# Delta rule and feed-forward on one core: chunk 0's substitution of four units in one ring instead of two pairs

## The chip, the cores and the metric

The kernel runs on one core of one Trainium2 chip. The metric is the time of one execution on the device, in microseconds (us). A core has a matrix engine (TensorE, PE in the profile; PEld is its loading of weights), VectorE (DVE), ScalarE (ACT), GpSimd (POOL) and SyncE (SP), which in this kernel only issues copies. GpSimd and ScalarE issue copies too. [...]

## What is computed

The inputs are q, k, v of 4 batches, 8 heads, 768 steps and 48 features, a step size beta for each step, and two weight matrices in 64-bit floats, w_in (384 x 2048) and w_out (2048 x 384). The reference, cut to what matters:

```python
k_n = k / (norm(k, axis=-1) + 1e-06)
state = zeros(B, H, D, D)
for t in range(S):
    y[:, :, t] = q[:, :, t] @ state                      # before the update
    v_old = k_n[:, :, t] @ state
    state += beta[:, :, t] * outer(k_n[:, :, t], v[:, :, t] - v_old)
x = y, with the heads side by side                       # (B*S, 384)
h = x @ w_in
out = (h * sigmoid(1.702 * h)) @ w_out                   # (3072, 384), f32
```

The recurrence is along the 768 steps; heads and batches are independent.

## The kernel before

The steps are cut into 6 chunks of 128. A chunk of one batch, with its 8 heads, is a unit; there are 24, numbered so that units 0 to 3 are the four batches of chunk 0, 4 to 7 those of chunk 1, and so on. Two units of neighbouring batches form a pair, whose 256 rows go through the feed-forward together.

Inside a chunk the recurrence becomes a triangular system. For each unit the kernel needs these things:

- Keys: `load` (line 84) fetches them, `normalize_first` or `normalize_mixed` (line 317) divides them by their norms: a square on ScalarE, a sum on VectorE, a power on GpSimd, then a product on VectorE. `turn` (line 385) transposes them on TensorE (psT, copied to kT), and `gram` (line 362) multiplies them with themselves (psG, copied to G).
- The inverse of the four 32 x 32 diagonal blocks of each head. `prepare` (line 389) writes the blocks of G to device memory (Nd) and gathers them again, so that each of the 128 partitions of NT holds one block of one unit. `invert` (line 444) then inverts all of them at once by a long row of products and sums on VectorE, scales them by beta (YS), and sends them through device memory (Yd) to tiles XB, in which TensorE can use them. Chunk 0 has its own way to NT: `diagonal` (line 428) computes only the diagonal blocks, and the code at lines 906 to 921 writes and gathers them.
- Scores: `scores` (line 558) transposes the queries and multiplies them with the keys (psT, psQ, copied to QS and M); `select` zeroes the upper triangle of M on GpSimd.

The substitution of a unit has four blocks (`blk`, 32 rows each). `solve` multiplies the values V of a block with the inverse (psU), `solved` copies the result to U on ScalarE, `below` multiplies U with the blocks of G below (psR), and `rest` subtracts that from V on VectorE. `together` (line 786) issues one set: the solves and the belows that it is given, head by head in turns on TensorE, then the copies, then the subtractions. Behind it, `queries` and `outputs` make the unit's rows of x (psY) and the state for the next chunk, and copy both out; the features that lie in other partitions are moved by six small copies on SP (xT<-last) once a pair is complete.

The feed-forward has two stages: `hidden` (line 693) computes x @ w_in (ph) and its gelu (gT), two features blocks of 128 at a time, and yields twice in each; `written` and `both_written` multiply with w_out (po). The weights come as 64-bit floats. `fetch_in` and `fetch_out` load them in pieces, w_in in four quarters of the features, and `conversions` (line 255) turns them into 32-bit floats with five instructions on VectorE and one on ScalarE for each piece; `fill(n)` issues n steps of it. `warm(n)` (line 132) issues n matmuls whose result is not used.

The order of the instructions is written out by hand: `pinned` (line 100) keeps nearly all in the order of the code. In the stage around the change (lines 933 to 1045) it is this:

1. Chunk 0 is inverted (line 945) while the scores of its four units are made. Sixty unused matmuls are tied to the end of the inversion by a memset (line 510).
2. Units 0 and 1 are substituted by `hops`: eight sets in which the two units take turns. Behind each set come one step of conversion, one step of the generator `keys` and eleven or three unused matmuls (lines 988 to 992). Their outputs follow, then the loads of the keys of units 7 and 8.
3. Units 2 and 3 are substituted in the same way, and `hidden` of the first pair runs between their sets. `keys` (line 964) prepares the keys of units 4 to 8 in steps during both.
4. `hidden` of the second pair is put behind that of the first; chunk 1 is inverted (lines 1033 to 1042) while `feed` issues the rest of x @ w_in.
5. From line 1047 on, `woven` takes the units of the later chunks one by one and weaves feed-forward work between them.

Of the kernel before, what the change touches and what calls it, by code (L numbers as in the profile page):

```python
# [18 lines left out]
def kernel(  # L19
# [21 lines left out]
    B, H, S, D = q.shape  # L41
# [15 lines left out]
    XR = DP - D  # L57
    NW, NA, NY, NU = 80, 3, 60, 11
    NQ = DFF // 4
# [71 lines left out]

    def warm(n, after=None):
        ps = ps_moe.tile([128, 256], F32, tag="moe", name="ps_warm")
        if after is not None:
            after(ps[:, 0:1], 0.0)
        for _ in range(n):
            pe.matmul(ps, lhsT=ones[:, 0:128], rhs=ones, start=True, stop=True)
# [35 lines left out]

    def fetch_in(i, other=None):

        f = slice(i * NQ, (i + 1) * NQ)
        raw = quarter(i if i < 3 else 4)
        for j in range(KC):
            for p, r, m, step in x_rows:
                (other if other and p >= DP else sync)(  # L180
                    out=as_rows(raw[j])[p : p + m, 0],
                    in_=moe_w_in[r + j * step : r + j * step + m, f],
                )
# [71 lines left out]
    def conversions():  # L255
# [27 lines left out]
    fetches = {  # L283
        ("in", 0, 1): lambda: fetch_in(3),
        ("in", 1, 1): lambda: (fetch_out(4), fetch_out(5), fetch_out(6), fetch_out(7)),
# [158 lines left out]
    def invert(c, b0=0, nb=B):  # L444
# [55 lines left out]
        for i in range(0, HS, Q):  # L500
# [7 lines left out]
            yield 0.0  # L508
        if c == 0:
            warm(NY, vec.memset)  # L510
        YS = wk.tile([128, BS, BS], F32, tag="P", name="YS")[part]
# [26 lines left out]
    class Step:  # L538
# [6 lines left out]
        def __init__(self, n, xT):  # L545
            self.c, self.b = units[n]
            self.xT = xT
            self.kn, self.kT, self.G = ready.pop(n)
            self.qp = QP[n % len(QP)]
            self.n, self.V = n, loaded.pop(n)  # L550
            self.US = late_U if n == B - 1 else US[n % len(US)]
            self.U = self.US[:, 0 : H * D].rearrange("p (h d) -> p h d", h=H)
            self.scored = self.scores()
# [4 lines left out]
        def scores(self):  # L558

            c, S = self.c, slice(128, 128 + D)  # L560
            self.QS = (
                spare("QS")[:, 0 : NP * (128 + D)].rearrange("p (j t) -> p j t", j=NP) if self.n == B - 1
                else wk.tile([128, NP, 128 + D], F32, tag="QS", name="QS", bufs=3)
            )
            transposed(self.qp, self.QS[:, :, 0:128])
            if c > 0:
# [3 lines left out]
            self.M = (  # L570
                spare("M").rearrange("p (h t) -> p h t", h=H) if self.n in (B - 1, B + 1)
                else wk.tile([128, H, 128], F32, tag="M", name="M", bufs=3)
# [119 lines left out]

    def hidden(xT, gT, t, cost):

        n = t.stop - t.start
        for f0 in range(0, FC, 2):
            if f0 // FQ == len(gT):
# [87 lines left out]

    def together(solves, belows):

        solves = [(X, blk) for X, blk in solves if X]
        belows = [(X, blk) for X, blk in belows if X]
        psU = bank("psU") if solves else None  # L790
        psR = bank("psR") if belows else None
        for h in range(H):
            for X, blk in solves:
                X.solve(blk, h, psU)
            for X, blk in belows:
                X.below(blk, h, psR)
        for X, blk in solves:
            X.solved(blk, psU)
        for X, blk in belows:
            X.rest(blk, psR)  # L800
# [89 lines left out]
    for i in range(B, len(KN)):  # L890
# [8 lines left out]
        for name in ("blocks", "others")  # L899
    ]  # L900
    quarter(2)
    late_U = spare("U")[:, 0 : H * D + XR]
    pool.memset(late_U[:, H * D :], 0.0)
    Nd = dram.tile([B * H * C * BS], F32, tag="Nds", name="Nd", bufs=1)
    turn(0)
    for b in range(B):
# [4 lines left out]
        if b % 2 == 1:  # L911
            for e in range(2):
# [3 lines left out]
                )  # L916
            d = slice((b - 1) * NB * H, (b + 1) * NB * H)
            sync(
                out=NT[d].rearrange("d i k -> d (i k)"),
                in_=Nd.rearrange("(d r) -> d r", r=BS * BS)[d],  # L920
            )
    pool.tensor_copy(landed[64:], NT[64:, 0, 0:1])
    for b in range(B):
# [12 lines left out]
    pair = [new_step(n) for n in range(B)]  # L936
    inverting = invert(0)
    for n in range(B):
        next(pair[n].scored)
        warm(NA)  # L940
        run(pair[n].scored)
# [21 lines left out]

    def keys():

        def unit(n):
            yield from normalize_mixed(n)
            yield from prepare(n)

        begun[2 * B] = prepare(2 * B)  # L970

        def first(n):
            yield from normalize_mixed(n)
            next(begun[n])

        work = [unit(n) for n in range(B, 2 * B)] + [first(2 * B)]
        for t in range(26):
            for u, begin in enumerate((0, 3, 6, 14, 17)):
                s = t - begin
                if s >= 0 and s % 2 == 0:  # L980
                    next(work[u], None)
            yield
        for w in work:
            run(w)
# [12 lines left out]
    load(8, ((KN, k),), sync)  # L997
    for n in range(B, B + 2):
# [82 lines left out]
```

## Time and profile before

| what | us |
|---|---|
| median of three runs | 794.65 (794.42 to 795.07) |
| the profiled execution | 796.73 |
| its span on the core | 795.0 |
| TensorE busy | 759.3 |
| VectorE busy | 459.0 |
| ScalarE busy | 239.8 |
| GpSimd busy | 123.3 |

The span is the time from the first to the last instruction of the core. Busy time says how long an engine had something in hand, not that it was needed then. In a row of the timeline, the bracket at the end gives the time for which the engine had stood idle before and the instruction that ended the wait. A copy is shown on the queue that issued it; it lands later.

### The profile page before, as it was taken

How to read it: one execution, taken by the hardware profiler on the slowest of the kernel's cores; microseconds unless marked ns; L12 is line 12 of the kernel's file. 1: busy time of each engine (PE TensorE's matmuls, PEld its weight loads, DVE VectorE, ACT ScalarE, POOL GpSimd, SP SyncE). 2: the span in 40 equal slices, each digit the busy share in tenths (PEclk: the TensorE clock that was granted, in tenths of full speed). 3: DMA queues.
4: the chain of work that ended last, by engine and by line, in shares of the span. 5: the costliest groups of instructions: out<-in, count | busy, mean ns of one | idle time of the engine just before them, and what ended most of it. 6: DMA issues, size and time to landing. Idle time of an engine off the chain costs nothing.

```text
span 795.0 us, 18695 instructions
## 1 busy us (share of the span) xinstructions
PE 759.3 (96%) x8083; PEld 567.4 (71%) x8083; DVE 459.0 (58%) x945; ACT 239.8 (30%) x521; POOL 123.3 (16%) x128
## 2 busy tenths in 40 slices
PE   9679999878899999999999999999999999999998
PEld 7457778645668768768768768668678678677684
DVE  5796667998797656656666666666756530100000
ACT  4432563234333323223223323223223223121120
POOL 4112320001222211211212212212210000000000
PEclk9678899999999999999999999999999999999999
DMA  6968462064334223222222231231230020000000
GB/s 124 147 122 187 120 132 65 13 173 103 89 79 94 54 62 65 55 68 59 54 69 58 55 86 41 64 89 29 64 86 12 21 43 1 12 16 1 26 0 20
DMA packets 139329, 52.81 MB, mean 66 GB/s; under 512 B 113824, under 2 KB 134432, under 8 KB 139248
## 3 DMA queue, kind: packets, MB, share of 16 engines
q1 hardware_dynamic: 136976, 43.70, 25.1%
q0 software_dynamic: 2176, 7.67, 3.8%
q8 instruction: 63, 1.03, 0.6%
q10 hardware_dynamic: 96, 0.26, 0.1%
q14 instruction: 18, 0.15, 0.1%
HBM read 33.13 MB, written 17.30 MB: 63 GB/s over the span
## 4 chain that ended last, share of the span: by engine, by line
PE 78%; DVE 14%; DMA 4%; issue 1%; ACT 1%; SPq 1%; DVEq 0%; POOL 0%; ACTq 0%; POOLq 0%
PE po L102 28%; PE ph L102 25%; PE psY L102 6%; PE psU L102 5%; DVE P L102 4%; PE ps_warm L102 3%; PE psQ L102 3%; DVE YB L102 3%; PE psG L102 3%; PE psT L102 2%; PE psR L102 2%; DVE w_out L102 2%; DVE NT L102 2%; DVE tmp L102 1%; SPq L102 1%
## 5 line engine op out<-in xcount | busy, mean ns | idle before, releaser
L102 PE MATMUL po<-w_out,gT 128*128 128x384 f32 x768 | 264.7, 492 | 5.9 <-DVE w_out L102 5.2
L102 PE MATMUL ph<-xT,w_in 128*128 128x256 f32 x1152 | 261.8, 383 | 3.2 <-ACT gT L102 2.8
L102 PEld LDWEIGHTS ph<-xT,w_in 128*128 128x128 f32 x1152 | 214.7, 190 | 36.0 <-ACT gT L102 4.7
L102 PEld LDWEIGHTS po<-w_out,gT 128*128 128x128 f32 x768 | 140.7, 190 | 96.5 <-DVE w_out L102 8.0
L102 DVE TENSOR_TENSOR V<-V,psR 64x384 f32<-64x384 f32 (+1 forms) x96 | 53.3, 556 | 197.2 <-PE psR L102 195.9
L102 ACT ACTIVATE gT<-ph 128x512 f32<-128x512 f32 x96 | 56.3, 596 | 136.6 <-PE ph L102 136.5
L102 DVE TENSOR_TENSOR P<-NT,YB 64x8 f32<-64x8 f32 (+31 forms) x190 | 88.8, 467 | 5.3
L102 ACT COPY US<-psU 32x384 f32<-32x384 f32 x92 | 43.2, 469 | 146.7 <-PE psR L102 130.0
L102 DVE TENSOR_REDUCE YB<-P 64x4 f32<-64x8 f32 (+31 forms) x190 | 80.9, 426 | 6.5
L102 PEld LDWEIGHTS psU<-V,XB 32*32 32x32 f32 x1536 | 58.7, 107 | 34.6 <-issue 26.7
L102 PE MATMUL psU<-V,XB 32*32 32x48 f32 x1536 | 69.8, 205 | 0.7 <-issue 0.3
L598 POOL TENSOR_SCALAR_AFFINE_SELECT M<-M 128x1024 f32<-128x1024 f32 x20 | 26.1, 1305 | 262.3 <-DVE M L102 168.8
L102 PE MATMUL psR<-US,G 32*32 32x48 f32 x2208 | 62.0, 205 | 1.6 <-issue 1.6
L102 PE MATMUL ps_warm<-ident 128*128 128x256 bf16 x275 | 44.4, 320 | 13.2 <-ACT G L102 7.2
L102 PEld LDWEIGHTS psR<-US,G 32*32 32x32 f32 x2208 | 52.3, 106 | 2.8 <-issue 2.3
L102 PEld LDWEIGHTS <-ident 128*128 128x128 bf16 x275 | 29.6, 113 | 22.0 <-issue 12.7
L102 PE MATMUL psQ<-QS,kT 48*128 48x176 f32 (+1 forms) x384 | 34.9, 322 | 1.1 <-ACT QS L102 1.1
L102 DVE TENSOR_TENSOR P<-NT 64x256 f32<-64x256 f32 (+7 forms) x40 | 33.7, 842 | 0.3
L102 DVE TENSOR_REDUCE NT<-P 64x64 f32<-64x1024 f32 (+7 forms) x40 | 32.6, 815 | 1.4
L87 POOL DMA_DIRECT2D KN<-in_k_dram x15 | 14.2, 947 | 112.2 <-PE psY L102 103.3
L102 PEld LDWEIGHTS psQ<-QS,kT 48*128 48x128 f32 x384 | 28.6, 192 | 4.0 <-ACT QS L102 2.4
L102 PE MATMUL psG<-kT 48*128 48x128 f32 x384 | 30.5, 303 | 0.2
(96 smaller groups left out, 602.0 us busy)
## 6 DMA issues: line engine op xcount, KB each, us to landing
Nd<-G SPq DMA_DIRECT2D x16, 512.0 KB, 3.5
QP<-in_q_dram SPq DMA_DIRECT2D x24, 192.0 KB, 3.7
V<-in_v_dram SPq DMA_DIRECT2D x24, 192.0 KB, 3.2
out_dram<-o SPq DMA_DIRECT2D x24, 192.0 KB, 2.1
XB<-Yd SPq DMA_DIRECT2D x24, 128.0 KB, 3.1
KN<-in_k_dram POOLq DMA_DIRECT2D x15, 192.0 KB, 3.8
Yd<-YS SPq DMA_DIRECT2D x22, 128.0 KB, 2.4
NT<-Nd SPq DMA_DIRECT2D x20, 128.0 KB, 2.6
```

The costliest lines, as they stand in the source:

```text
L87: dma(out=dst[n % len(dst)][:, :, 0:D], in_=src[b, :, c * C : (c + 1) * C, :].rearrange("h p d -> p h d"),)
L102: return lambda *a, **kw: tc.keep_in_program_order(op(*a, **kw))
L598: (pool if self.n < B else nc.gpsimd).affine_select(out=self.M, in_=self.M, compare_op=ALU.is_gt, fill=0.0, base=0, pattern=[[0, H], [1, 1 ...
```

## The change

- Chunk 0's four units are substituted in one ring of 16 sets: set i solves block i // 4 of unit i % 4, and multiplies and subtracts what set i - 2 solved. `together` takes something to issue between the copies and the subtractions (`beside`): one step of conversion in every fourth set, and in others a step of the preparation of the keys of units 4, 5 and 6, by the table `aside`.
- The outputs of units 0 to 3 follow sets 13, 14 and 15 and the ring. No unused matmuls stand between the sets; 90 stand before the last part of chunk 0's inversion, without the memset.
- The turns and products of the keys of units 4, 5 and 6 follow the ring, and only then come the loads of the keys of units 7 and 8. Units 7 and 8 are prepared between the steps of x @ w_in.
- `hidden` takes a range of features. Both pairs run behind the ring, first features 0 to 7 of each, then 8 to 15. The number of steps that `feed` issues during the inversion of chunk 1 is changed accordingly.
- Chunk 0's blocks are gathered into NT by one copy for all four units instead of two for two each.
- Quarters 2 and 3 of w_in are fetched through GpSimd's queue, quarter 2 directly behind quarter 1 and quarter 3 at set 12, instead of through SP behind the inversion and behind the conversion of quarter 0.
- The buffers of unit 3 (U, QS, M) are taken from the spare buffers at once, ahead of those for quarter 2.

The diff, without its changed constants (NW, NA, NY = 80, 3, 90; NU is gone):

```diff
-    def warm(n, after=None):
+    def warm(n):
         ps = ps_moe.tile([128, 256], F32, tag="moe", name="ps_warm")
-        if after is not None:
-            after(ps[:, 0:1], 0.0)
...
-    def fetch_in(i, other=None):
+    def fetch_in(i, other=None, only=False):
...
-                (other if other and p >= DP else sync)(
+                (other if other and (only or p >= DP) else sync)(
...
     fetches = {
-        ("in", 0, 1): lambda: fetch_in(3),
...
-        if c == 0:
-            warm(NY, vec.memset)
...
-            self.US = late_U if n == B - 1 else US[n % len(US)]
+            self.US = late["U"][:, 0 : H * D + XR] if n == B - 1 else US[n % len(US)]
...
-    def hidden(xT, gT, t, cost):
+    def hidden(xT, gT, t, cost, part=range(0, FC, 2)):
 
         n = t.stop - t.start
-        for f0 in range(0, FC, 2):
+        for f0 in part:
...
-    def together(solves, belows):
+    def together(solves, belows, beside=iter(())):
...
         for X, blk in solves:
             X.solved(blk, psU)
+        for _ in beside:
+            pass
         for X, blk in belows:
             X.rest(blk, psR)
...
+    late = {name: spare(name) for name in ("U", "QS", "M")}
     quarter(2)
-    late_U = spare("U")[:, 0 : H * D + XR]
...
-            d = slice((b - 1) * NB * H, (b + 1) * NB * H)
-            sync(
-                out=NT[d].rearrange("d i k -> d (i k)"),
-                in_=Nd.rearrange("(d r) -> d r", r=BS * BS)[d],
-            )
-    pool.tensor_copy(landed[64:], NT[64:, 0, 0:1])
+    sync(out=NT.rearrange("d i k -> d (i k)"), in_=Nd.rearrange("(d r) -> d r", r=BS * BS))
+    pool.tensor_copy(landed, NT[:, 0, 0:1])
...
     fetch_in(1, other_queue)
+    fetch_in(2, other_queue, True)
     fill(6)
...
+    warm(NY)
     run(inverting)
-    for s in pair:
+    for s in four:
         s.select()
-    fetch_in(2)
     fill(5)
-
-    def hops(a, b):
-
-        yield [(a, 0)], []
-        for blk in range(NB - 1):
-            yield [(b, blk)], [(a, blk)]
-            yield [(a, blk + 1)], [(b, blk)]
-        yield [(b, NB - 1)], []
...
-    preparing = keys()
-    path = hops(*pair[:2])
-    for i in range(2 * NB):
-        together(*next(path))
+    norms = {n: normalize_mixed(n) for n in range(B, 2 * B + 1)}
+    begun.update((n, prepare(n)) for n in range(B, 2 * B + 1))
+
+    def tick(*ns):
+        for n in ns:
+            if next(norms[n], True):
+                next(begun[n], None)
+
+    aside = [(), (4,), (), (4,), (), (4, 5), (), (5,), (), (5, 6), (), (6,), (), (6,), (), ()]
+    for i in range(B * NB):
+        j = i - 2
+        together(
+            [(four[i % B], i // B)],
+            [(four[j % B], j // B)] if j >= 0 and j // B < NB - 1 else [],
+            iter([fill(1) if i % 4 == 2 else tick(*aside[i])]),
+        )
+        if i >= B * NB - 3:
+            put_out(four[i - (B * NB - 3)])
+        if i == 12:
+            fetch_in(3, other_queue, True)
+    put_out(four[3])
+    for n in (4, 5, 4, 6, 5, 6):
+        tick(n)
         fill(1)
-        ahead_of(preparing, 1)
-        warm(NU if i < 6 else NA)
-    for s in pair[:2]:
-        put_out(s)
-        fill(1)
-    load(7, ((KN, k),), sync)
-    load(8, ((KN, k),), sync)
+    for n in (7, 8):
+        load(n, ((KN, k),), sync)
...
-    ffn.append(hidden(xTs[0], gTs[0], slice(0, NTH), 1.3))
-    path = hops(*pair[2:])
-    for i in range(2 * NB):
-        together(*next(path))
-        if i > 2:
-            feed()
-        else:
-            warm(NU // 2)
-        fill(2)
-        ahead_of(preparing, 2)
+    for part in (range(0, FC // 2, 2), range(FC // 2, FC, 2)):
+        for i in range(2):
+            ffn.append(hidden(xTs[i], gTs[i], slice(0, NTH), 1.3, part))
+    xTs.pop(0), xTs.pop(1)
+    aside = [(7, 4), (5,), (7, 6), (8,), (7,), (8,), (7,), (8,), (7,), (8,), (7,)]
+    for i in range(16):
+        feed()
+        fill(2 if ("in", 3, 1) not in done else 0)
+        if i < len(aside):
+            tick(*aside[i])
         if 3 <= i < 6:
             fetch_out(i - 3)
-    for s in pair[2:]:
-        put_out(s)
-        feed()
-        fill(2)
-    ffn.append(hidden(xTs[1], gTs[1], slice(0, NTH), 1.3))
-    xTs.pop(0), xTs.pop(1)
-    run(preparing)
...
-        feed(2 if i >= 16 else 1 - i % 2)
+        feed(1 if i >= 16 or i % 3 == 2 else 0)
```

More of the change, by code (lines that the diff above doesn't have):

```diff
@@ L57 @@
     XR = DP - D
-    NW, NA, NY, NU = 80, 3, 60, 11
+    NW, NA, NY = 80, 3, 90
     NQ = DFF // 4
@@ L561, in scores @@
             self.QS = (
-                spare("QS")[:, 0 : NP * (128 + D)].rearrange("p (j t) -> p j t", j=NP) if self.n == B - 1
+                late["QS"][:, 0 : NP * (128 + D)].rearrange("p (j t) -> p j t", j=NP) if self.n == B - 1
                 else wk.tile([128, NP, 128 + D], F32, tag="QS", name="QS", bufs=3)
@@ L570, in scores @@
             self.M = (
-                spare("M").rearrange("p (h t) -> p h t", h=H) if self.n in (B - 1, B + 1)
+                (late["M"] if self.n == B - 1 else spare("M")).rearrange("p (h t) -> p h t", h=H)
+                if self.n in (B - 1, B + 1)
                 else wk.tile([128, H, 128], F32, tag="M", name="M", bufs=3)
@@ L900 @@
     ]
+    late = {name: spare(name) for name in ("U", "QS", "M")}
     quarter(2)
-    late_U = spare("U")[:, 0 : H * D + XR]
-    pool.memset(late_U[:, H * D :], 0.0)
+    pool.memset(late["U"][:, H * D : H * D + XR], 0.0)
     Nd = dram.tile([B * H * C * BS], F32, tag="Nds", name="Nd", bufs=1)
@@ L935 @@
         warm(NA)
-    pair = [new_step(n) for n in range(B)]
+    four = [new_step(n) for n in range(B)]
     inverting = invert(0)
     for n in range(B):
-        next(pair[n].scored)
+        next(four[n].scored)
         warm(NA)
-        run(pair[n].scored)
+        run(four[n].scored)
         warm(NA)
@@ L962, in put_out @@
         steps.pop(s.n)
[L964 to L984, printed above, removed]
-    preparing = keys()
-    path = hops(*pair[:2])
-    for i in range(2 * NB):
-        together(*next(path))
-        fill(1)
-        ahead_of(preparing, 1)
-        warm(NU if i < 6 else NA)
-    for s in pair[:2]:
-        put_out(s)
-        fill(1)
-    load(7, ((KN, k),), sync)
-    load(8, ((KN, k),), sync)
+    norms = {n: normalize_mixed(n) for n in range(B, 2 * B + 1)}
[19 more added lines that the diff above has]
+        tick(n)
+        fill(1)
+    for n in (7, 8):
+        load(n, ((KN, k),), sync)
     for n in range(B, B + 2):
```

## The prediction

> **What bounds the kernel now.** I read the busy slices first, then the stretches by stage, then the chain of waits around the place that the change touches, then the timeline of VectorE and of the two queues there. In the page:
>
> ```profile
> span 795.0 us, 18695 instructions
> PE   9679999878899999999999999999999999999998
> DVE  5796667998797656656666666666756530100000
> ```
>
> TensorE is full from about slice 10 (200 us) to the end, so the kernel ends when TensorE got its long tail started. What decides when the tail starts lies before 200 us. Here are the stretches (columns: stretch; length; busy time and instructions of TensorE, its weight loads, VectorE, ScalarE, GpSimd; granted clock; DMA share; GB/s):
>
> ```profile
> 64.80:90.60 25.80, 24.23 (x478) 19.20 (x478) 14.96 (x28) 8.77 (x20) 3.90 (x3) 0.80 0.48 114
> 90.60:119.30 28.70, 26.76 (x500) 21.48 (x500) 20.15 (x40) 18.27 (x36) 9.28 (x11) 1.00 0.72 173
> 129.60:157.00 27.40, 24.78 (x126) 21.23 (x125) 26.02 (x54) 7.22 (x15) 1.41 (x1) 1.00 0.00 1
> 165.30:205.00 39.70, 33.68 (x364) 21.18 (x364) 33.92 (x72) 17.23 (x36) 4.16 (x3) 1.00 0.51 138
> 300.00:700.00 400.00, 399.77 (x4442) 299.67 (x4438) 228.68 (x480) 112.36 (x247) 64.73 (x52) 1.00 0.22 51
> ```
>
> From 129.6 to 157 VectorE works 26.0 of 27.4 us: that is the inversion of chunk 1. Behind it VectorE converts w_out and TensorE waits for it (33.7 of 39.7 us). So from 129.6 to about 205 VectorE sets the pace, and then TensorE has no slack (399.8 of 400). A later start of the inversion is therefore a later end, nearly one for one. Why it starts at 129.6 is in VectorE's and SP's timelines (start, us, what, idle before and who ended it):
>
> ```profile
> 124.56 0.96 DVE L102 SCALAR_TENSOR_TENSOR w_in<-tmp,w_in 128x768 f32<-128x768 f32 x1
> 129.59 1.23 DVE L102 TENSOR_TENSOR NT<-NT,bI 128x1024 f32<-128x1024 f32 x1 [4.07 <-DMA NT<-Nd]
> ```
> ```profile
> 94.48 1.17 SPq L102 DMA_DIRECT2D KN<-in_k_dram  x2
> 114.85 1.90 SPq L102 DMA_DIRECT2D Nd<-G  x4
> 119.86 0.31 SPq L102 DMA_DIRECT2D NT<-Nd  x1
> 120.22 1.96 SPq L102 DMA_DIRECT2D Nd<-G  x4
> 126.02 0.52 SPq L102 DMA_DIRECT2D NT<-Nd  x1
> ```
>
> VectorE has nothing left and waits 4.07 us for the last blocks (NT) of unit 7, the last of chunk 1. They took the whole way: keys loaded at 94.5, normalized, turned, multiplied, written (Nd), gathered (NT). **The question is when that way ends in the changed kernel.** The chain of waits shows what the old substitution cost:
>
> ```profile
> 64.84 0.79 PE psU L102 x16
> 67.75 1.31 PE ps_warm L102 x11
> 71.55 1.57 issue
> 77.34 2.46 PE ps_warm L102 x11
> ```
>
> Its sets of pair 0 run at a pace set by eleven dummy matmuls each: 1.31 us at full clock (119 ns each), 2.46 us at half (224 ns).
>
> [...] in pair 0 the clock stayed halved for about 10 us (73.8 to 84.4) although TensorE was hardly idle[...]
>
> **The change part by part**, in time of the profiled execution: 796.73 us, of which the span is 795.0. The runs' median is 794.65, 2.1 under it.
>
> *Gather of chunk 0 in one copy.* NT was fetched in two copies of 256 KB (median 3.7 us); four of 128 KB took 2.9. So 0.8 us per 128 KB gives 5.3 us for 512 KB, an estimate. SP issues the last Nd write some 0.5 us sooner, as the early gather at 21.6 is gone: landing at about 25.9 + 5.3 = 31.2 instead of 30.3. Inversion 0 and all behind it, up to XB at 64.8, come 1.0 us later: 65.8 (bounds 64.8 if size costs nothing, 67.3).
>
> *Fetches moved from SP to GpSimd.* Quarter 2: 12 issues of some 0.5 us (6 took 2.99) on GpSimd, behind quarter 1, in its 23.3 us of idling before the gate; the 1.5 MB fill DMA time idle from 52 to 58.5. Nothing; without that cover up to 2 us on XB. Quarter 3: 12 issues at set 12, behind the last pow of the ring; needed at E+24 below, so nothing; GpSimd's next work behind it, four fetches of w_out and the pow of unit 7 at E+19, comes later than it lands.
>
> *ph in halves.* Both pairs' features 0 to 7 come first, 48 matmuls that need only quarters 0 and 1 of w_in; quarters 2 and 3 are converted meanwhile. As many matmuls as before, so nothing, as long as VectorE's conversions (E+36 below) end ahead of their use at about E+38. The spare buffers named earlier, and the memset of 0.06 us that leaves VectorE: nothing, no step waits for them.
>
> *Dummy matmuls.* 87 leave the substitution (14.5 us busy from 64.8 to 119.3). The 90 that replace the pinned 60 no longer wait for VectorE: they start at 51.3 and last 90 x 0.119 = 10.7 us, to 62. TensorE then stands 3.8 us, so the ring starts at half clock.
>
> *The ring.* A set takes TensorE 0.8 us at full and 1.43 at half clock (75.84 to 77.27). Sets 0 and 1: 2 x 1.43 = 2.9. Each set with block 0 has two updates on VectorE (1.14) and a fill or part of a normalization ahead of it (mean of 0.96, 0.54, 0, 0.93 is 0.61): 4 x 1.75 = 7.0. Blocks 1 and 2: VectorE 0.56 + 0.61 is under 1.43, so 8 x 1.43 = 11.4. Sum 21.3, at 87.1 (full clock: VectorE's 1.2 rules, 17.5). Four outputs with sets 14 and 15: 1.4 us each (64 rows, 2.81 for two), and the third and fourth bank must be emptied by ScalarE (1.4 us): 8.6 at full, 12.6 at half clock; I take 10.4. The ring ends at E = 97.5 (bounds 91 and 101). Before, pair 1's last output ended at 119.3, so substitution is 22 us shorter; but 82 of 192 matmul records of ph (0.22 us each) were done by 129.6, and the keys of chunk 1 were prepared in its gaps.
>
> *From E to the inversion of chunk 1.* In the new order the last three units' psT and psG stand behind the ring, and keys of unit 7 are loaded behind all 12 Nd writes on SP, where before they were loaded at 94.5, ahead of them. The queries and values of units 4 and 5 stand behind these keys; they are first used in the inversion, and have 20 us.
> 1. Turn and multiply units 4, 5, 6 through two ps_big buffers, TensorE and ScalarE by turns (psT 0.6, kT 0.6, psG 1.1, G 1.08, three times, first after 1.4 of xT copies): 10.3 at full, 13.5 at half clock; 11.5.
> 2. Nd of unit 6 on SP 2.1, keys land 4.6 (median; 3.5 to 6.8): E+18.2.
> 3. ScalarE has the square of unit 7 ahead of the first gelu: 0.52, table load 1.28, gelu 0.60: E+20.6. TensorE filled both ps_moe buffers (12 matmuls) by E+17 and stands. The 9 ph matmuls ahead of psT of unit 7: 4.0 at full, 8.0 at half; 5.0: E+25.6. The normalization (0.54 + 1.66 pow + 0.93) hides under them, at E+23.
> 4. psT 0.6, six ph 2.65, psG 1.1: E+30.0. ScalarE's gelu, one conversion and G: 1.3: E+31.3.
> 5. Four Nd writes to landing 5.1 (114.85 to 119.9), NT 3.5: E+39.9.
> VectorE's 25 fills and the keys of 7 and 8 end at about E+36, so they hide; 4 us is their margin.
>
> The inversion starts at 97.5 + 39.9 = 137.4 instead of 129.6: **+7.8 us**. Behind it nothing new: ph still to do is some 21 us (24.4 before), over by E+63, before the first po at 29.5 us behind the inversion's start (159.2 before); the 3 us saved go into idling. The profiled execution would take 804.5 (span 802.8), and the median, 2.1 under it, **802.5 us**.
>
> **Rivals.**
> *Small loss.* The clock holds through the ring (E about 92 to 94), then +2 to +5: 797 to 800. For it: the outputs of pair 0 ran at full clock (2.81 for two). Against: the dummies are gone.
> *Large loss.* Half clock to the first ph, keys at 6.8 us, a late psG: terms 1 to 3 at their upper ends add 2 + 2.2 + 3 and the ring 3 to the 7.8, 18 in all: 813.
> *Faster.* The new order does what it removes: with E = 92 and lower ends (10.3 + 1.9 + 3.5 + 2.4 + 4.0 + 4.2 + 1.2 + 5.0 + 2.9 = 35.4) the inversion starts at 127.4: 792.5. It decides once E plus the way is under 128. For it: SP no longer waits for each unit's Nd before the next (5.4 us per unit from 103.5 on). Against: it needs all lower ends at once.
> *No change.* Inversion at 128 to 131.2, midway: 794.5.
>
> **How the numbers follow.** Forecast (+5 to +12) 0.45, small loss 0.22, large loss 0.18, no change 0.06, faster 0.09. Within 0.2% (1.6 us) is about what a measurement of this kernel can't tell from no change. Slower by more: 0.85; within 0.06; faster 0.09. The range leaves 0.1 at each end: 795.5 to 811. The forecast's own range is 799.5 to 806.5.
>
> **What would show it.** NT<-NT,bI of chunk 1 at about 137, released by the copy of NT; VectorE idle 3 to 5 us ahead of it. Keys of unit 7 issued on SP near 111, behind 12 Nd writes. Ring sets 1.4 us apart with a clock near half; last output near 97. A gap on TensorE after 12 ph matmuls, ended by gelu. Wrong if the way of unit 7 is under 33 us, or if po takes over the start of the tail because ph is done earlier than VectorE's conversions allow.

## The result: slower, and the profile after

The changed kernel takes 808.28 us (median; runs from 806.47 to 809.76), beside 794.86 us for the kernel before on the same chip: a ratio of 1.0164, with a 95% interval of 1.0135 to 1.0194. It is slower by 13.4 us. The forecast was 802.5 us, within 795.5 to 811. The measured time lies inside that range, but outside the forecast's own part of it (799.5 to 806.5), between it and the large loss.

The profiled execution took 806.47 us, 1.8 under its kernel's median; the one of before lay 2.1 over its own. So the two traces differ by less than the medians do: the spans by 9.6 us. The two traces can explain only that; the rest is taken up below.

The page of the changed kernel, the span and the busy slices of TensorE and VectorE with the granted clock:

```profile
span 804.6 us, 18577 instructions
...
PE   9697959878899999999999999999999999999998
...
DVE  5886447999797667567666666656656630100000
...
PEclk9676588999999999999999999999999999999999
```

What is new lies in slices 4 to 6: the clock (PEclk, in tenths) reads 6, 5 and 8 there, where it was 8, 8 and 9 before, and TensorE has a dip in the sixth slice (101 to 121 us). The stretches show both (columns as before: stretch; length; busy time of TensorE, weight loads, VectorE, ScalarE, GpSimd; clock; DMA share; GB/s):

```profile
66.00:90.00 24.00, 20.32 (x623) 18.85 (x624) 16.03 (x32) 8.81 (x19) 10.17 (x14) 0.52 0.17 43
90.00:100.00 10.00, 9.90 (x125) 9.29 (x122) 1.97 (x5) 3.50 (x12) 0.78 (x2) 0.61 0.35 75
...
110.00:120.00 10.00, 3.03 (x13) 2.39 (x12) 1.49 (x3) 2.94 (x5) 1.77 (x1) 0.74 1.09 162
120.00:139.10 19.10, 19.10 (x92) 16.12 (x92) 14.79 (x25) 9.01 (x16) 4.27 (x6) 0.87 0.62 142
139.10:167.00 27.90, 24.14 (x122) 20.30 (x120) 26.25 (x53) 6.62 (x14) 1.59 (x1) 1.00 0.00 1
...
300.00:700.00 400.00, 399.78 (x4410) 300.19 (x4407) 234.73 (x483) 114.46 (x250) 68.19 (x54) 1.00 0.23 53
```

The ring (66 to 90) and its outputs (90 to 100) run at about half clock. From 110 to 120 all three compute engines stand: TensorE works 3.0 of 10 us, VectorE 1.5, ScalarE 2.9. From 139 on the picture is that of before again: the inversion of chunk 1 on VectorE, 26 of 28 us. VectorE's timeline gives its start:

```profile
134.00 0.96 DVE L102 SCALAR_TENSOR_TENSOR w_in<-tmp,w_in 128x768 f32<-128x768 f32 x1
134.88 0.35 DVE L102 TENSOR_SCALAR tmp<-raw 128x384 int32<-128x384 int32 x1
139.16 1.23 DVE L102 TENSOR_TENSOR NT<-NT,bI 128x1024 f32<-128x1024 f32 x1 [3.93 <-issue]
```

The inversion starts at 139.16 instead of 129.59, 9.57 us later, and the span is 9.6 us longer. From its start to the end of the span it is 665.4 us in both traces. So behind the start of the inversion this execution took as long as that of before, and all that was lost was lost ahead of it. The bracket names no releaser here (`issue`); the next lines show that the blocks of unit 7 came last. SP's timeline shows their way:

```profile
93.90 10.49 SPq L102 DMA_DIRECT2D xT<-last  x12
104.48 9.11 SPq L102 DMA_DIRECT2D Nd<-G  x12
113.69 1.02 SPq L102 DMA_DIRECT2D KN<-in_k_dram  x2
...
131.67 2.81 SPq L102 DMA_DIRECT2D Nd<-G  x4
135.82 0.31 SPq L102 DMA_DIRECT2D NT<-Nd  x1
```

The gather of its blocks is issued at 135.82, and the fastest of the four gathers of chunk 1 takes 3.3 us to land, which gives 139.1, when the inversion starts. Its keys are issued at 113.69 (94.48 before), behind twelve copies of x and twelve block writes. ScalarE's timeline shows what waits for them:

```profile
117.03 0.52 ACT L102 ACTIVATE ksq<-KN 128x384 f32<-128x384 f32 x1 [8.95 <-DMA KN<-in_k_dram]
117.57 1.28 ACT L102 ACT_TABLE_LOAD   x1
118.86 0.60 ACT L102 ACTIVATE gT<-ph 128x512 f32<-128x512 f32 x1
```

ScalarE waits 8.95 us for these keys. The first gelu of x @ w_in is queued behind the square of unit 7 and runs at 118.86, though all matmuls of ph issued so far had ended at 112.55, and TensorE, whose two ph buffers are full, stands for 6.97 us until that gelu has emptied one. In TensorE's timeline each matmul of ph is two records (1152 in the whole trace for the kernel's 576), so the 24 records are the 12 matmuls that fill both buffers:

```profile
107.10 5.45 PE L102 MATMUL ph<-xT,w_in 128*128 128x256 f32 x24
119.52 6.88 PE L102 MATMUL ph<-xT,w_in 128*128 128x256 f32 x18 [6.97 <-ACT gT L102]
```

### The profile page after: what moved, and what is told of

Same layout as the page of the kernel before. It is cut to its first block, busy times and chain, and to the rows that moved or that the text cites. A ratio compares the mean times of both kernels' runs of the same rounds, so it can differ in the third digit from the quotient of the medians.

```text
span 804.6 us, 18577 instructions
## 1 busy us (share of the span) xinstructions
PE 763.6 (95%) x8026; PEld 575.6 (72%) x8026; DVE 458.5 (57%) x944; ACT 240.1 (30%) x521; POOL 137.0 (17%) x152
## 4 chain that ended last, share of the span: by engine, by line
PE 76%; DVE 14%; DMA 5%; issue 2%; ACT 2%; SPq 1%; DVEq 0%; POOL 0%; ACTq 0%; POOLq 0%
PE po L102 28%; PE ph L102 25%; PE psY L102 6%; PE psU L102 5%; DVE P L102 4%; PE psQ L102 3%; PE psR L102 3%; DVE YB L102 3%; PE psG L102 2%; PE psT L102 2%; DVE w_out L102 2%; DVE NT L102 2%; DMA Nd<-G 1%; DVE tmp L102 1%; DMA KN<-in_k_dram 1%
## 5 line engine op out<-in xcount | busy, mean ns | idle before, releaser
L102 PEld LDWEIGHTS psU<-V,XB 32*32 32x32 f32 x1536 | 63.8, 112 | 34.0 <-issue 27.6
L102 PE MATMUL psU<-V,XB 32*32 32x48 f32 x1536 | 74.4, 212 | 3.0 <-issue 1.7
L102 PE MATMUL psR<-US,G 32*32 32x48 f32 x2208 | 64.5, 210 | 1.4 <-ACT US L102 0.9
L102 PEld LDWEIGHTS psR<-US,G 32*32 32x32 f32 x2208 | 54.9, 110 | 3.0 <-ACT US L102 1.3
L102 PE MATMUL ps_warm<-ident 128*128 128x256 bf16 x218 | 31.6, 303 | 8.6 <-ACT G L102 7.2
L102 PEld LDWEIGHTS <-ident 128*128 128x128 bf16 x218 | 22.7, 107 | 13.9 <-issue 8.2
```

The lines of the kernel that those rows point to most:

```text
L102: return lambda *a, **kw: tc.keep_in_program_order(op(*a, **kw))
```

## The experiments

Each was run beside the kernel before on the same chip; the groups used four chips. The median of before lay between 793.3 and 795.9 us, so ratios are compared, not times across groups of runs. "Start" is the start of the inversion of chunk 1 in the profiled execution: 129.59 before, 139.16 after.

### Unit 7's keys earlier

```diff
         if i >= B * NB - 3:
             put_out(four[i - (B * NB - 3)])
+        if i in (13, 14):
+            load(i - 6, ((KN, k),), sync)
...
-    for n in (7, 8):
-        load(n, ((KN, k),), sync)
```

> The changed kernel, with one edit: the loads of the keys of units 7 and 8 are issued by SP right behind the outputs of units 0 and 1 (about 89 and 93 us), ahead of the copies of x and of the twelve Nd writes, instead of at 113.7. Theory A (the way of unit 7's keys starts the inversion of chunk 1 late): the square of unit 7 no longer waits at 117 but runs at 108, the stand of TensorE behind 12 ph matmuls (7.0 us) is gone, the inversion starts at about 130 instead of 139.2, and the time falls by 8 to 10 us to 798.5 to 800. Theory B (the half clock of the ring is what costs): the keys are not what is waited for; a change under 2 us. Theory C (fetches and the gather): no change.

Measured: 800.31 us (22 runs), ratio 1.0075 (1.0052 to 1.0098) where the changed kernel has 1.0164: 0.89% less, some 7 us. The start is 131.39, 7.8 earlier. SP's timeline of this run:

```profile
89.67 0.37 SPq L102 DMA_DIRECT2D KN<-in_k_dram  x1
94.61 4.45 SPq L102 DMA_DIRECT2D xT<-last  x6
...
105.36 7.95 SPq L102 DMA_DIRECT2D Nd<-G  x12
...
123.52 1.80 SPq L102 DMA_DIRECT2D Nd<-G  x4
128.96 0.31 SPq L102 DMA_DIRECT2D NT<-Nd  x1
```

The keys are issued at 89.7 and are there when the square of unit 7 comes up on ScalarE (108.8, no wait); the stand of TensorE is gone. So the place of one small load in SP's queue was worth some 7 of the 13.4 us. Time and start move by nearly the same amount, as the prediction's one-for-one rule says.

### Dummies put back into the ring

```diff
             iter([fill(1) if i % 4 == 2 else tick(*aside[i])]),
         )
+        warm(7 if i < 6 else 5)
```

> The changed kernel with unused matmuls behind every set of the ring: seven in sets 0 to 5, five in the others. Theory B: the clock stays full through the ring (dummies of 0.12 us each fit into the gaps), the sets take 1.2 to 1.75 us instead of 1.9, each output 1.7 instead of 3.0, the last output ends at 91 to 93 instead of 99, and the time falls by 6 to 8 us to 800.5 to 802.5. Theory A: the end of the ring moves the way of unit 7 with it, so the same fall, but the way from the end of the ring to the inversion stays 40 us, and the stand of TensorE ahead of the first gelu stays 7 us or longer. If small tiles and five dummies don't hold the clock, the dummies cost 0.22 us each at half clock: up to 15 us slower.

Measured: a median of 820.52 us over six runs that fall apart: five take 817 to 827 us, with a mean clock of 0.946 to 0.954, and one takes 803.29, with 0.974. The stretches of the profiled execution (826.54 us):

```profile
66.00:90.00 24.00, 24.00 (x478) 17.17 (x478) 9.60 (x20) 5.45 (x12) 3.32 (x2) 0.50 0.03 5
90.00:100.00 10.00, 10.00 (x164) 7.40 (x161) 4.08 (x8) 2.81 (x5) 4.75 (x8) 0.50 0.19 52
100.00:110.00 10.00, 10.00 (x110) 8.22 (x110) 2.54 (x5) 1.75 (x5) 2.89 (x6) 0.50 0.49 110
```

TensorE is busy in every one of these 44 us and its clock is half in all of them. So in this execution the dummies did not bring the clock back; they only added their own length. The run at 803.29 is another matter: it is 5 us under the changed kernel and within 1 us of what theory B expected if the clock held, and its mean clock is near that of before. It was not profiled. So the dummies cure nothing reliably, but the experiment doesn't show that they never help, and what decides between the two outcomes is not known.

### Chunk 0 gathered in two copies

```diff
-    sync(out=NT.rearrange("d i k -> d (i k)"), in_=Nd.rearrange("(d r) -> d r", r=BS * BS))
-    pool.tensor_copy(landed, NT[:, 0, 0:1])
+            d = slice((b - 1) * NB * H, (b + 1) * NB * H)
+            sync(
+                out=NT[d].rearrange("d i k -> d (i k)"),
+                in_=Nd.rearrange("(d r) -> d r", r=BS * BS)[d],
+            )
+    pool.tensor_copy(landed[64:], NT[64:, 0, 0:1])
```

> The changed kernel with the gather of chunk 0 undone: two copies of 256 KB instead of one of 512 KB. The step of the prediction had the single copy 1.0 us later; the trace has it 1.6 us earlier (28.97 against 30.60). If the second is the gather's doing, the inversion of chunk 0 starts at about 30.5 again. Theory A and B: the time stays within 2 us of the changed kernel, 806 to 810, since SP, still issuing loads until 57.4, holds back the writes of the inverses whichever the start is.

Measured: 807.91 us, ratio 1.0158 (1.0114 to 1.0201): as the changed kernel. The first inversion starts at 30.25 instead of 28.97, so the single copy is the faster way by 1.3 us; the ring too begins 1.5 us later with two (65.69 against 64.15). In the times this doesn't show: the six runs spread over 4.6 us. This trace also shows what the last part of the difference may be. Its start is 137.94, 1.2 earlier than the changed kernel's, with the clock back during the outputs of the ring (1.00 from 92 to 100 us; 0.50 and 0.78 in the changed kernel), and yet its span is 4.4 us longer (809.0). The stretches behind the inversion:

```profile
178.00:214.00 36.00, 33.68 (x337) 21.32 (x338) 27.91 (x62) 14.29 (x32) 3.09 (x2) 0.86 0.47 121
214.00:248.00 34.00, 31.18 (x438) 20.64 (x442) 27.63 (x65) 9.76 (x26) 7.41 (x5) 0.90 0.29 67
```

The trace of the changed kernel has a clock of 1.00 in the same stretches. Here 14% of 36 us and 10% of 34 us, 8.4 us of full clock, are missing; in the changed kernel's trace TensorE idles only 6.8 of the 70 us from 179 to 249, so that it has little room to make up for them.

### Quarter 2 of w_in fetched on SP again

```diff
-    fetch_in(2, other_queue, True)
...
     for s in four:
         s.select()
+    fetch_in(2)
```

> The changed kernel with quarter 2 of w_in fetched by SP behind the inversion of chunk 0, as before, instead of by GpSimd behind quarter 1. Theory C (the fetch fills the copy engines and holds SP back): SP ends its loads at about 50 instead of 57.4, the writes of the inverses start at 55.5 and XB lands at about 61.5 instead of 64.2, so the ring and all behind it come 2.5 us earlier: 805 to 806. Against that the fetch then runs beside the ring, where little else is copied: no loss there. Theory A and B alone: no change by more than 1.5 us.

Measured: 803.86 us (six runs), ratio 1.0128 (1.0082 to 1.0173): 2.9 us off the changed kernel by the ratios, 4.4 by the medians. The two intervals overlap, so the time alone doesn't settle it. The start does move, by 5.0 us in the trace (134.19), and the queue shows why. SP's timeline of the changed kernel, from the loads ahead of the ring on:

```profile
39.42 9.40 SPq L102 DMA_DIRECT2D KN<-in_k_dram  x3
48.87 5.43 SPq L102 DMA_DIRECT2D bI<-in_beta_dram  x4
54.35 2.91 SPq L102 DMA_DIRECT2D w_out<-in_moe_w_in_dram  x6
57.36 0.83 SPq L102 DMA_DIRECT2D Yd<-YS  x2
61.34 2.35 SPq L102 DMA_DIRECT2D XB<-Yd  x4
```

and of this run:

```profile
39.37 2.25 SPq L102 DMA_DIRECT2D KN<-in_k_dram  x3
41.67 3.03 SPq L102 DMA_DIRECT2D bI<-in_beta_dram  x4
44.75 2.91 SPq L102 DMA_DIRECT2D w_out<-in_moe_w_in_dram  x6
55.23 0.78 SPq L102 DMA_DIRECT2D Yd<-YS  x2
57.32 2.68 SPq L102 DMA_DIRECT2D XB<-Yd  x4
```

The same three key loads take SP 2.25 us without quarter 2 in flight, and 9.40 with it. In the changed kernel SP is busy with loads until 57.3, and the inverse of chunk 0, ready at about 55.4, waits behind them; from the copy to Yd to that of XB it is then 4.0 us instead of 2.1. XB is issued 4.0 us late, and the ring begins 2.6 us late (64.15 against 61.59).

### Both undone together

```diff
-    fetch_in(2, other_queue, True)
...
+    fetch_in(2)
...
+        if i in (13, 14):
+            load(i - 6, ((KN, k),), sync)
...
-    for n in (7, 8):
-        load(n, ((KN, k),), sync)
```

> The changed kernel with two of its moves undone together: the keys of units 7 and 8 are loaded behind sets 13 and 14 of the ring, and quarter 2 of w_in is fetched through SP behind the selects of the scores. Each alone gave 800.3 and 803.9 us against 808.3. If the two act on different stretches (the fetch moves the start of the ring, the keys the way from the ring's end to the inversion of chunk 1), they add: 8.0 + 4.4, so 795 to 797 us, with the inversion of chunk 1 starting at 126 to 128. If both only take away the same stand of SP's queue, the time stays at about 800.

Measured: 798.45 us (22 runs), ratio 1.0044 (1.0024 to 1.0064). The start is 127.94, as expected if they add, and 1.65 earlier than before. The time is not as expected (795 to 797): it stays 3.5 us above before. The trace doesn't show this rest of about 0.4%: its span is 0.8 us shorter than that of before (794.2). What goes with the time is the clock. Each run has its mean clock, and span times (1 - clock) is the time that it lost to it: in these 22 runs 29 to 38 us (median 31.9), in the runs of before on this chip 10 to 24 (median 17.5). Within either kernel the runs' times go with it: a run that lost 1 us more took 0.6 us longer in this kernel and 0.8 in the one before (correlation 0.81 and 0.80).

The traces show where the clock is lost. From 66 to 100 us, the ring and its outputs, the nine traces of orders with the ring lose 11.9 to 17.0 us, and the four traces with the old substitution 0 to 5.0. This part lies ahead of the inversion, so it is already in the start and is no second cost. From 140 to 250 us both kinds lose some in some traces: 0 to 10.0 us and 0 to 5.2. Whether the rest of 0.4% comes from there stays open.

### The keys of units 4 and 5 inside the ring as well

```diff
-    aside = [(), (4,), (), (4,), (), (4, 5), (), (5,), (), (5, 6), (), (6,), (), (6,), (), ()]
+    aside = [(), (4,), (), (4,), (), (4, 5), (), (5, 4), (4,), (5, 6), (), (6, 5), (5,), (6,), (), (6,)]
...
             put_out(four[i - (B * NB - 3)])
+            fill(2)
...
-    for n in (4, 5, 4, 6, 5, 6):
+    for n in (7, 6, 7, 4, 5, 7):
...
-    aside = [(7, 4), (5,), (7, 6), (8,), (7,), (8,), (7,), (8,), (7,), (8,), (7,)]
+    aside = [(8,), (7, 6), (8,), (7,), (8,), (7,), (8,), (8,)]
```

(and the two moves of the run before)

> As the run with both moves, and in addition the turns and products of the keys of units 4 and 5 (and the turn of unit 6) stand inside the ring, as in the order of before, with two more steps of conversion behind each set of outputs. If the way of unit 7 sets the start of the inversion of chunk 1 in this order too, what is taken off it (10 us of turns and products between the ring and unit 6's block writes) brings the inversion to 120 to 124, although the ring itself ends 3 to 4 us later: 788 to 794 us, at or under the kernel before. If TensorE's own work is the bound by then (the ring at half clock plus the work put into it), the ring is longer by all that left the way behind it: 795 to 797, no gain on the run with both moves.

Measured: 798.6 us (21 runs), ratio 1.0056 (1.0035 to 1.0076), with the start at 130.06. The last step of unit 8 came one too early here: its blocks went into NT over those of unit 4, ahead of the inversion, which waited for them and then inverted the wrong blocks for unit 4. The next run, with that step taken out, is the one to read.

> The run with all moved, but unit 8's blocks are no longer gathered ahead of the inversion of chunk 1 (there they overwrote the blocks of unit 4 in NT, which changed the first heads of chunk 1, and the inversion waited for them until 130.06). Unit 7's blocks were issued at 123.91 there, so the inversion starts at 126 to 127, 3 to 4 us earlier: 795 to 796 us. If the start of the inversion no longer decides, the time stays at 798 to 799.

Measured: 796.31 us (14 runs), ratio 1.0011 (0.9993 to 1.0029); start 126.14, where it was expected. Its profiled execution took 799.92 us, though, 3.6 over the median: with the start 3.5 us earlier than before its span is 3.2 longer (798.2), and TensorE's clock is 0.91 from 140 to 215 us, where that of before has 1.00. One step further:

```diff
-            iter([fill(1) if i % 4 == 2 else tick(*aside[i])]),
+            iter([tick(*aside[i]), fill(1 if i > 7 or not aside[i] else 0)]),
...
-    for n in range(B, B + 2):
-        load(n, ((QP, q),), sync)
-    for n in range(B, B + 2):
-        load_values(n, sync)
...
-    aside = [(8,), (7, 6), (8,), (7,), (8,), (7,), (8,)]
+    aside = [(7,), (6, 7), (7,), (), (8,), (8,), (8,), (8,)]
...
+        if i == 2:
+            for n in range(B, B + 2):
+                load(n, ((QP, q),), sync)
+            for n in range(B, B + 2):
+                load_values(n, sync)
```

> The order of the run with all moved, with three more moves: unit 7 is turned and multiplied at once behind the ring, ahead of everything of unit 8; the queries and values of units 4 and 5 are loaded behind unit 7's blocks; and eight steps of conversion more stand in the ring. If the way of unit 7 and then VectorE's conversions (95% busy from 96 to 122 us in the trace of the run with all moved) set the start of the inversion of chunk 1, both end near 118: inversion at 117 to 121 instead of 126 to 130, and 788 to 793 us, under the kernel before. If the ring at half clock is VectorE's or TensorE's bound, the steps put into it lengthen it by as much as they save behind it: inversion at 124 to 127, 794 to 797 us.

Measured: 794.75 us (22 runs), ratio 1.0000 (0.9983 to 1.0017). The start lies between the two expectations, the time in the second: 122.64, 7 us earlier than in the kernel before, and no faster than it. In the profiled execution (span 791.0, so 4.0 shorter for a start 7.0 earlier) part of this can be followed. TensorE's stretches from 10 us behind the start on, a row of VectorE's timeline, and TensorE's timeline at the first product with w_out:

```profile
132.64:142.64 10.00, 10.00 (x54) 8.59 (x55) 8.90 (x13) 3.24 (x6) 0.00 (x0) 1.00 0.00 0
142.64:152.64 10.00, 10.00 (x54) 8.51 (x52) 9.23 (x13) 3.04 (x7) 1.09 (x1) 1.00 0.01 2
152.64:162.64 10.00, 6.48 (x32) 3.40 (x32) 9.62 (x22) 3.26 (x5) 0.00 (x0) 1.00 0.92 221
```
```profile
142.96 0.42 DVE L102 TENSOR_TENSOR V<-V,psQ 128x96 f32<-128x96 f32 x2 [1.04 <-PE psQ L102]
```
```profile
154.63 1.53 PE L102 MATMUL po<-w_out,gT 128*128 128x384 f32 x4 [1.85 <-ACT gT L102]
```

TensorE works through all of the 30 us behind the start and still begins po only 32.0 us behind it (29.6 before). It still has ph to do, and VectorE, in the middle of the inversion, waits for a product of the first unit's scores (psQ) that stands among it. So with the start this early, TensorE's own backlog takes over as the bound, at a price of 2.4 us here. That the ring at half clock left this backlog is likely, but no run shows it. The rest, up to the median, I put down to the clock: these runs lose a median of 31.7 us to it, those of before beside them 17.5. That is a reading of the run list, not an experiment.

### Parts of the change in the kernel before

The single gather alone, in the kernel before:

```diff
-            d = slice((b - 1) * NB * H, (b + 1) * NB * H)
-            sync(
-                out=NT[d].rearrange("d i k -> d (i k)"),
-                in_=Nd.rearrange("(d r) -> d r", r=BS * BS)[d],
-            )
-    pool.tensor_copy(landed[64:], NT[64:, 0, 0:1])
+    sync(out=NT.rearrange("d i k -> d (i k)"), in_=Nd.rearrange("(d r) -> d r", r=BS * BS))
+    pool.tensor_copy(landed, NT[:, 0, 0:1])
```

> The kernel before with one part of the change alone: chunk 0's blocks are gathered into NT by one copy of 512 KB instead of two of 256 KB. The prediction charged this with 1.0 us; the trace of the changed kernel shows the first inversion 1.6 us earlier. If the single copy is the faster way and nothing absorbs it, the first inversion starts at 29.0 instead of 30.6 and the time is 0.5 to 1.6 us under the kernel before (ratio 0.998 to 0.9995). If it is absorbed by SP's queue of loads ahead of the blocks' way to the substitution, the ratio is 1.000 within its interval. By the prediction's price it would be 1.001.

Measured: 793.17 us (22 runs), ratio 0.9973 (0.9949 to 0.9997). The first inversion starts at 29.20 instead of 30.60. VectorE's first subtraction of the substitution starts 2.0 us earlier (65.85 against 67.84), which agrees with the 0.27% of the ratio (2.1 us). (The inversion of chunk 1 starts at 124.23, 5.4 earlier; the other 3.4 go with the clock: from 66 to 90 us this trace lost 1.7 us to it and that of before 5.0.) So this part of the change is a small gain, just clear of the noise.

The other part of the change's order that speaks for it is that SP issues the block writes of several units one behind the other. Before, SP issues unit 6's gather (119.86) only when unit 6's writes have landed (from 100 to 130 us it waits 8.2 us in all for such writes), and unit 7's writes are queued behind that gather. This put into the kernel before, with unit 7's preparation begun one step sooner (13 for 14 in the last line; the two are not separated):

```diff
+            gathers.append((b, Nd))
+            if b == B - 1:
+                for j, N in gathers:
                     sync(
-                out=NT[b * NB * H : (b + 1) * NB * H].rearrange("d i k -> d (i k)"),
-                in_=Nd.rearrange("(d r) -> d r", r=BS * BS),
+                        out=NT[j * NB * H : (j + 1) * NB * H].rearrange("d i k -> d (i k)"),
+                        in_=N.rearrange("(d r) -> d r", r=BS * BS),
                     )
...
-            for u, begin in enumerate((0, 3, 6, 14, 17)):
+            for u, begin in enumerate((0, 3, 6, 13, 17)):
```

> The kernel before with SP's order in chunk 1 changed alone (block writes of the four units first, then their gathers; chunk 0 gathered in two copies as before). Inversion of chunk 1 at 125 to 126 instead of 129.6, behind VectorE's last conversion. One for one down to there: 790 to 791.5 us (ratio 0.995 to 0.996). If TensorE's backlog already sets the end: 793.5 to 795 us (ratio 0.998 to 1.000).

Measured: 791.76 us (22 runs), ratio 0.9954 (0.9926 to 0.9982). SP's and VectorE's timelines:

```profile
96.21 12.83 SPq L102 DMA_DIRECT2D Nd<-G  x16
109.08 1.86 SPq L102 DMA_DIRECT2D NT<-Nd  x4
113.86 3.69 SPq L102 DMA_DIRECT2D xT<-last  x6
```
```profile
119.19 1.22 DVE L102 TENSOR_TENSOR NT<-NT,bI 128x1024 f32<-128x1024 f32 x1
```

All 16 writes go out in a row, the four gathers follow, and VectorE comes to the inversion without a wait, where it stood 4.07 us before. The start is 10.4 earlier than in the trace of before, but 6.2 of this lie ahead of the edit: the copies of the first pair's x are already issued at 84.46 instead of 90.63. TensorE's clock from 70 to 90 was 1.00 in this execution, and 0.71 and 0.78 in the two halves of that stretch before; a single trace has such luck in it, and medians over many runs have less. Measured from those copies, the start comes 4.2 earlier, which agrees with the 0.46% of the ratio (3.7 us).

And with the single gather:

> The kernel before with chunk 0's blocks gathered in one copy, and with SP's order in chunk 1 changed: the block writes of all four units first, then their four gathers (before, each unit's gather waits on SP for its writes to land, 5.4 us a unit, and unit 7's writes, ready at 114.6, are issued at 120.2). VectorE's conversions end at about 121 to 125, so the inversion of chunk 1 can start there, 4 us earlier than with the one gather alone. If the start of the inversion sets the end one for one: 788.5 to 790.5 us (793.2 with the one gather alone). If TensorE's own backlog sets the end once the inversion starts before about 126, as the run with unit 7 first suggests (inversion 7 us earlier than in the kernel before, the same time): 792 to 794 us.

Measured: 789.16 us (22 runs), ratio 0.9923 (0.9899 to 0.9947), start 116.58. It is faster than both kernels. The two edits add, as far as the intervals tell (0.27 and 0.46 against 0.77%), so in the kernel before the start still decides where it is at 117: po begins at 146.62, 30.0 us behind it. TensorE's backlog, which took over in the changed order at 122.6, has hardly taken over here.

## Why the prediction was right, and which terms were not

**The rule.** "A later start of the inversion is a later end, nearly one for one": 9.57 against 9.6 us in the two traces. By the ratios, with the keys undone the time fell 7.1 us for 7.8 us of start; with the fetch undone 2.9 for 5.0; with both 9.5 for 11.2. It held, nearly. It failed in the last order of the ring (start 122.64), where TensorE's backlog took its place, and in traces with a lower clock behind the start: from the start to the end it is 665.4 us before and after, and 672.1 in the run with the start at 126.14.

**The way of unit 7.** Keys behind all the block writes, the stand of TensorE behind the gelu, then psT, psG, blocks and gather: each step came in the predicted order, with the predicted signs: a gap of TensorE behind 12 ph matmuls, ended by the gelu, and VectorE idle for 3.93 us ahead of the inversion. In time behind the end of the ring, E = 99.0: keys landed at E+18.0 (predicted 18.2), first gelu done at E+20.5 (20.6), psG of unit 7 done at E+31.4 (30.0), inversion at E+40.2 (39.9). The run with the keys earlier shows that this was the cause and not a companion of it.

**Terms that were off.** Three ran against each other.

- *Gather in one copy.* Predicted 1.0 us later, measured 1.6 earlier: the 512 KB landed 3.6 us after their issue, as the 256 KB had (3.7), where the sum took 5.3 from the step between 128 and 256 KB; and the issue itself came 1.4 earlier (25.07 against 26.47), not 0.5.
- *Fetches moved to GpSimd.* "Nothing; without that cover up to 2 us on XB." This is the cost that was put at nothing and was not. The fetch was in flight with SP's own loads (its issues end at 44.8), and SP took 9.4 us over three loads that take 2.25 without it. Without it XB is issued 4.0 us earlier, and the time falls by some 3 us, with a wide interval. It also swallowed what the gather had won: the ring started at 64.15, 0.6 ahead of before; with the fetch undone it starts 3.2 ahead.
- *The ring.* Sets 0 to 13 ended at 86.1 (87.1). The outputs with sets 14 and 15 were taken at 10.4, between full and half clock; they ran at half clock but for the last us and took 12.9. The upper end of the prediction, 12.6, leaves the two sets at half clock (2.9) out of its sum. E came 1.5 us later than predicted. The nine ph matmuls ahead of psT of unit 7 (the 18 records above) took 6.7 us and not 5.0, again by the clock (0.75 from 120 to 130 us).

The sum of these came out at 9.6 instead of 7.8 for the start, much closer than its terms, and that is luck: without the fetch the ring would have started 4.2 us ahead of the prediction (61.59 against 65.8), the fetch took back 2.6, and the sets and outputs another 3.2.

**Right by another way: the half clock of the ring.** The prediction had the 90 dummies end at 62, TensorE stand for 3.8 us, and the ring start at half clock for that reason. The traces have such stands. In that of before TensorE stands 4.61 us ahead of the sixty dummies (51.26 to 55.87); its clock falls from 1.00 to 0.50 at 53.7, within the stand, and is back at 1.00 at 60.5. Ahead of the ring it stood 3.35 us in the run with the keys earlier and 4.65 in the one with two gathers, and the first 31 matmuls of the ring took 2.62 and 2.65 us; in the run with the dummies it stood 3.09 us, and the first 16 took 0.86, as in the changed kernel. There, in TensorE's timeline and stretches, no such stand comes before the fall of the clock:

```profile
53.04 10.33 PE L102 MATMUL ps_warm<-ident 128*128 128x256 bf16 x93
64.15 0.86 PE L102 MATMUL psU<-V,XB 32*32 32x48 f32 x16 [0.78 <-DMA XB<-Yd]
```
```profile
64.00:68.00 4.00, 3.64 (x160) 3.24 (x160) 1.77 (x3) 1.89 (x5) 0.00 (x0) 0.88 0.47 66
68.00:72.00 4.00, 1.94 (x82) 1.76 (x86) 2.44 (x6) 1.21 (x3) 1.68 (x1) 0.50 0.02 4
```

The dummies last to 63.4, TensorE stands 0.78 us, and the ring starts at full clock. The clock halves at 67.0, in set 3, without a longer stand in the 10 us before. So the half clock was forecast, but the stand that was to cause it did not happen. Why the clock fell is open.

**What was missing.** The prediction laid the shift between two traces on the median of before. The medians are 13.4 apart and not 9.6, so the forecast is 5.8 us short, 1.8 by the start and the rest by this step. The changed kernel's runs lie at two levels, 806.5 to 807.0 and 809.6 to 809.8. The upper two lost 37 to 38 us to the clock, the lower two 34.6. In the trace of the two-gather run such a loss lies behind the inversion; it can also lie ahead of it: the run with the writes first has the order of before up to the first copies of x, and in its trace these come 6.2 us earlier than in that of before. Whether orders with the ring lose more behind the inversion no run settles; that they lose some 30 us and more in all, and before 17.5 to 19, is measured, and the traces show a large part of the difference in the ring and its outputs.

**The rivals.** "Small loss" needed the clock to hold through the ring; it didn't, and the dummies that were to hold it (second run) made things worse in five runs of six. "Faster" named the right mechanism, that SP no longer waits for each unit's writes before the next: put into the kernel before, it is worth 0.46%. The changed kernel threw it away by placing unit 7's keys behind those writes. "Large loss" asked for 18 us; its half clock came, its late keys did not.

## What to carry to other kernels

When an order is rewritten, list for each queue what now stands ahead of the one item that the next stage waits for: a single load of 192 KB, put behind 24 small copies, cost 7 to 8 us here. A copy moved to another queue to fill "idle" DMA time can still hold up the first queue's own loads: with quarter 2 in flight from GpSimd's queue, SP took 9.40 us over its three key loads and 2.25 without it, and as SP carries the critical copy here, XB was issued 4.0 us late. And a part of a losing change can be a gain: take the parts one by one back to the kernel before.

## What the runs showed of the hardware that was not expected

- In one execution TensorE kept half clock for 44 us of work without a gap in the trace (matmuls of 32 x 32 tiles with dummies of 128 x 256 between them, 66 to 110 us, clock 0.50). In the changed kernel the clock fell from 1.00 to 0.50 at 67.0, though TensorE had not stood longer than 0.78 us in the 10 us before, and stayed near half for the ring and its outputs (0.52 from 66 to 90 us, 0.61 from 90 to 100).
- One gather of 512 KB landed as soon as one of 256 KB (3.6 us in the changed kernel against 3.7 before).
- Three loads of 192 KB held SP for 2.25 us or, with 1.5 MB in flight from GpSimd's queue, for 9.40.
